# Another load order in the prologue and another order of all steps, in a kernel that adds a long convolution and a gated MLP

## The chip, the cores and the metric

The kernel runs on one NeuronCore of a Trainium2 chip. The metric is the device time of one execution in microseconds. A core has TensorE (PE, matmuls; its weight loads are shown as PEld), VectorE (DVE), ScalarE (ACT), GpSimd (POOL) and SyncE (SP), which here issues nearly all DMA transfers. Each engine works through its own instructions in order; semaphores connect them.

## The reference

S = 2048 positions, D = 640, F = 1728, all in bf16. `xn` is the layer norm of x; the output is the sum of x, a gated long convolution of `k` and `v`, and a gated MLP of `xn`.

```python
x  = A_q
xn = _layernorm(x, axis=-1)
# A: short convolution of k (4 taps), times v, then a causal convolution of length S per channel
k_shift = sum(k_pad[:, t:t + S, :] * shift_k[:, ks - 1 - t] for t in range(ks))
kv = k_shift * v
y  = irfft(rfft(kv, 2 * S) * rfft(ssm_k, 2 * S))[:S] + kv * ssm_D
A  = xn * y
# B: gated MLP
B  = (sigmoid(xn @ w_gate) * (xn @ w_up)) @ w_down
out = x + A + B
```

## The kernel before

**Layout.** Position s = 16 p + b sits on partition p in block b, so x is a tile of 128 partitions x 16 blocks x 640. The MLP goes over four groups of four blocks (512 positions each); the convolution goes over five chunks of 128 channels. The Fourier transform of a chunk is done by matmuls with tables, in two stages with a transposition through DRAM between them, and so is the inverse.

**MLP, per group.** `ln_*` make the statistics and `xn` on VectorE (the power -1/2 on GpSimd); `xn_mm` transposes the blocks on TensorE, `xn_ev` copies them to `xnT` on ScalarE. For each of 13 column blocks `fc` of 128, `gate_mm` and `up_mm` are five matmuls of 512 columns each (lines 257); `gate_ev` is the sigmoid on ScalarE (266), `up_ev` the product into `hT` on VectorE (272). The last 64 columns of gate and up share one product (`both_mm` 278, `both_ev`, `both_mul`, which writes `hT[13]`). `down_mm` (296) multiplies `hT` by `wd`, each output half in two parts of seven matmuls; the second part needs `hT` 7 to 13. `down_ev` (301) adds the result to x.

**Convolution, per chunk c.** `load_h`, `load_halo`, `load_k`, `load_v`, `load_taps` bring `hn`, `kx`, `kvh`, `sraw`. `h_turn` transposes the filter on VectorE, `add_D` adds D on GpSimd, `taps` reorders the taps into `sc`. `kv_op` 0 to 15 (VectorE, 329 to 338) are the short convolution and the product with v, eight steps for each half of the blocks. Then: `st1_mm` 0 to 7 (355, 357) into a PSUM tile, copied by `st1_ev` on ScalarE into a `t1` tile (two steps fill one; there are two `t1` buffers), `wr1` writes `t1` to DRAM (`d1`), `rd2` reads it back as `t2`, `st2_mm` (388), `st2_ev`, `prod` (401, 403), `inv1_mm` (417), `inv1_ev`, `wr2`, `rdb`, `inv2_mm` (456) and `inv2_q`, `inv2_x`, which add the chunk's part to x. `store` writes x to the output.

**PSUM.** Pool psG has four buffers in rotation: gate, up, down, transposed blocks of groups 1 to 3, `psb`. Pool psC has two: stage tiles of the convolution, and the prologue's transposed blocks.

**The prologue (469 to 508).** x's block 0 is loaded on SP's queue, block 1 and then blocks 2 and 3 on ScalarE's; the first 256 columns of `w_gate` on SP's and of `w_up` on ScalarE's, columns 256 to 512 of both on SP's. `busy(15)` issues 15 matmuls of 512 columns on a tile of zeros, whose result nobody reads. Four blocks go through statistics and `xn` on VectorE in order; `ln_xn` of block i - 1 stands behind `ln_stats` of block i. `turn(i)` transposes block i and copies it. For group 0 the products of column blocks 0 and 1 are done in quarters, one for each block as it comes: `quarter(u, fc, i)`, with u = 0 for gate and 1 for up.

**The order of everything else.** `chains` holds a list of steps for each letter; `ORDER` is a string of letters, and each letter issues the next step of its list. So `ORDER` sets the order of the instructions on every engine. The letters: `m` and `n` the loads listed at 540 to 562 (SP); `Z` and `t` taps; `g` MLP matmuls, `s` sigmoids, `u` VectorE's part of the MLP; `l`, `P`, `e`, `E` layer norm, its power, transposition and copy; `H`, `D`, `k` filter, D and `kv_op`; `a`, `A`, `w` stage 1, its copy and its write; `r`, `b`, `B`, `p` read back, stage 2, its copies and the spectral product; `c`, `C`, `W`, `R`, `d`, `q` the inverse; `h`, `K`, `V`, `T` loads of later chunks; `o` stores.

**Transfers in flight.** The trace shows eight semaphores for the transfers of SP and ScalarE in rotation; a transfer is issued when the one eight places before it has landed.

Of the kernel before, what the change touches and what calls it, by code (L numbers as in the profile page):

```python
# [22 lines left out]
NFC = 14  # L23
# [34 lines left out]
def kernel(  # L58
# [410 lines left out]
    sync.dma_start(x[:, 0, :], xr[:, 0, :])  # L469
    nc.scalar.dma_start(x[:, 1, :], xr[:, 1, :])  # L470
    nc.scalar.dma_start(x[:, 2:4, :], xr[:, 2:4, :])
    for u in range(2):
        load_w((sync, nc.scalar)[u], 0, 256, u)
# [15 lines left out]
    busy(15)  # L489
# [10 lines left out]
    for i in range(4):  # L500
        for fc in range(2):
            for u in range(2):
                quarter(u, fc, i)
            if (i, fc) in ((0, 0), (1, 0), (1, 1)):
                turn(1 + i + fc)
# [34 lines left out]
    for k in ((load_w, sync, 512, 768, 0),  # L540
              (load_w, sync, 512, 768, 1),
              (load_taps, 0),
              (sync.dma_start, SMt[:], SMd.ap()),
              (load_w, sync, 768, 1024, 0),
              (load_w, sync, 768, 1024, 1),
              (load_w, sync, 1024, 1280, 0),
              (load_w, sync, 1024, 1280, 1),
              (load_wd, sync, 0, 7),
              *ks(0),
              (load_w, sync, 1280, FF, 0),  # L550
              (load_w, sync, 1280, FF, 1),
              *hs(0),
              *vs(0),
              (load_wd, sync, 7, NFC),
              (sync.dma_start, S1t[:], S1d.ap()),
              *hs(1),
              (load_x, sync, 1),
              *ks(1),
              *vs(1)):
# [62 lines left out]
    mmmmmmmmmmZgmgsmgumgsmgugsgugsmgugskgkugkskgumkgsmkgumkgsmTguHgsHDgumgskkgukgskmgukgskgumkgkmgmutmkm  # L622
    auTaAHgAHDagAwlhauaAlglaglguwlgkPkgAulgAllleKeuKwEekaEekaEgkEVVHAgAHDgwughkgkugkskguKrrkaskaAgkAkguw
    gkskgutkgTskgkKuKaksaAKkgAkaugAwkaksaAkgkwakAgVuAVHasgwHDAauhgAkgkskwbugBrkgBkktbgpBrTkgBpsapsaAuguA
    apKgKswAkaugAkaKkwsakgVHAVgAuDHgswkcugCkgkskCgnuWakaAkgAkgukwbguBrlgBlgulbgBrlgBuglkPpgnulgllleenuEe
    kbEeprgEEgptkBgupBgkaauAgpAkapgswAkaugAkawksaAgkAkguwlcsglCgClbusgrlBWgBkugslpPkaauAgllAlglspwbgBruR
    kgBkscpguCpgCksWbkgBrugBkksbpgBrudBpdgsRqpcqgCqugCqpsWbgBrukgBspbgBrupdBadqsaApRgqAqapgwAqauseeEueaE
    egEEgAgAwaudAdqgwqRqcugCqgCguWbgBrgBugpbpdBrdqgBuqgqpcqgCupgCguWbgBrgBugpspRbgBrugBspcguCpgsCguWbsdr
    BdqgRBqqguqbpsgrBpgBugpspcgCugCsWbguBrdBgqspbqgBupgBspgucpsdCgRqRCqguWbsgBgBugpspgudsdqcqgCqoqdCudqg
    WqqgsqgugoguRRguggugguogodudqogqqogqdoudqogqqogqguogoouo  # L630
    """
    left = {k: iter(v) for k, v in chains.items()}
# [34 lines left out]
```

## Time and profile before

| | us |
|---|---|
| median of 3 runs | 239.67 (239.56 to 239.82) |
| profiled execution, device time | 239.41 |
| its span, first to last instruction | 237.6 |
| TensorE busy | 231.4 |
| VectorE busy | 190.3 |
| ScalarE busy | 141.2 |

The span is the part that the trace shows; about 1.8 us of the device time lie around it.

A row of the profile names the source line, the engine, the operation, what it writes and reads, and its time; a row in order of time begins with its start and its length. "Issue to landing" of a transfer is the time from the instruction on the queue to the semaphore that tells of the last byte. The page's groups give these durations: a product of 512 columns takes 1.08 us for five matmuls, one part of a down block 0.95, a transposed block 0.28, a step `a` 0.45.

### The profile page before, as it was taken

The numbers are of one execution on the slowest core, as the hardware profiler recorded it, in microseconds if no ns is written. First come the engines' busy times: TensorE is split into PE (matmuls) and PEld (weight loads), VectorE is DVE, ScalarE is ACT, GpSimd is POOL, SyncE is SP. The second block draws the span as 40 slices with busy tenths as digits, with TensorE's granted clock in tenths as the row PEclk, the third lists the DMA queues.
The fourth block names the chain that finished last, engine by engine and source line by source line (L and its number), as shares of the span: only waits on it lengthen the run. The fifth ranks groups of instructions, "written<-read, shape, count | busy, mean of one in ns | idle before, by whom it ended". The sixth has DMA issues, their size and how long they took to land.

```text
span 237.6 us, 5553 instructions
## 1 busy us (share of the span) xinstructions
PE 231.4 (97%) x2265; PEld 135.1 (57%) x2265; DVE 190.3 (80%) x350; ACT 141.2 (59%) x178; POOL 11.2 (5%) x24
## 2 busy tenths in 40 slices
PE   8799999999999999999999999999999999999994
PEld 2564445878556455667754434577664434456782
DVE  3633889999999999999999999865585695968372
ACT  2342331728559897864888887997558858764000
POOL 4210000020000000002001000000000000000000
PEclk9999999999999999999999999999999999999999
DMA  7999999889998999999444888975939795285674
GB/s 212 292 314 233 259 322 298 183 249 284 253 311 243 253 295 297 284 267 319 148 183 152 234 230 258 227 228 203 241 109 222 186 281 123 89 238 144 196 237 134
DMA packets 88975, 54.82 MB, mean 231 GB/s; under 512 B 47670, under 2 KB 83062, under 8 KB 88694
## 3 DMA queue, kind: packets, MB, share of 16 engines
q1 hardware_dynamic: 88006, 53.66, 80.8%
q10 hardware_dynamic: 944, 0.82, 1.1%
q8 instruction: 17, 0.28, 0.5%
q14 instruction: 8, 0.07, 0.1%
HBM read 36.12 MB, written 18.35 MB: 229 GB/s over the span
## 4 chain that ended last, share of the span: by engine, by line
PE 95%; DMA 3%; ACT 0%; DVE 0%; ACTq 0%; issue 0%
PE pd L296 26%; PE pg L257 23%; PE pu L257 23%; PE psb L456 4%; PE ps L357 4%; PE ps L355 4%; PE ps L388 3%; DMA w<-in_B_w_up_dram 3%; PE psa L417 2%; PE pg L278 2%; PE pt L234 2%; PE pu L248 1%; PE pg L248 1%; ACT xnT L223 0%; DVE x L301 0%; ACT L119 0%
## 5 line engine op out<-in xcount | busy, mean ns | idle before, releaser
L257 PEld LDWEIGHTS <-w 128*128 128x128 bf16 x500 | 46.5, 98 | 54.3 <-issue 5.3
L296 PE MATMUL pd<-wd,hT 128*128 128x320 bf16 x448 | 64.3, 299 | 0.0
L257 PE MATMUL pg<-xnT,w 128*128 128x512 bf16 x250 | 62.2, 379 | 0.0
L257 PE MATMUL pu<-xnT,w 128*128 128x512 bf16 x250 | 62.1, 379 | 0.0
L296 PEld LDWEIGHTS <-hT 128*128 128x128 bf16 x448 | 42.8, 98 | 17.8 <-issue 1.7
L266 ACT ACTIVATE sig<-pg 128x512 bf16<-128x512 f32 x52 | 31.3, 605 | 30.1 <-PE pg L257 28.2
L272 DVE TENSOR_TENSOR hT<-sig,pu 128x512 bf16<-128x512 bf16 x52 | 35.2, 679 | 14.7 <-PE pu L257 9.3
L223 ACT CAST t<-ps 128x1024 bf16<-128x1024 f32 x40 | 39.1, 1023 | 11.4 <-DMA d<-t 6.3
L223 ACT CAST xz<-ps 128x1024 bf16<-128x1024 f32 x40 | 38.6, 1018 | 10.6 <-PE ps L388 10.5
L301 DVE TENSOR_TENSOR x<-pd,x 128x320 bf16<-128x320 f32 x32 | 15.4, 480 | 15.8 <-PE pd L296 15.7
L403 DVE TENSOR_TENSOR xz<-xz 128x2048 bf16<-128x2048 bf16 x20 | 24.4, 1220 | 0.2
L357 PE MATMUL ps<-kvh,S1t 128*128 128x128 bf16 x160 | 21.2, 219 | 0.0
L335 DVE TENSOR_TENSOR acc<-acc,tmp 128x1024 bf16<-128x1024 bf16 x30 | 20.7, 689 | 0.7
L355 PE MATMUL ps<-kvh,S1t 128*128 128x128 bf16 x160 | 21.2, 217 | 0.0
L333 DVE TENSOR_TENSOR tmp<-kx,sc 128x1024 bf16<-128x1024 bf16 x30 | 20.6, 687 | 0.4
L223 ACT CAST ao<-psa 128x1024 bf16<-128x1024 f32 x16 | 15.6, 1014 | 5.6 <-PE psa L417 3.5
L461 DVE TENSOR_TENSOR yx<-psb,xn 128x512 bf16<-128x512 f32 x20 | 13.8, 691 | 3.9 <-PE psb L456 2.9
L355 PEld LDWEIGHTS <-S1t 128*128 128x128 bf16 x160 | 15.5, 97 | 2.3
L357 PEld LDWEIGHTS <-S1t 128*128 128x128 bf16 x160 | 15.3, 96 | 2.3
L223 ACT COPY xnT<-pt 128x640 bf16<-128x640 bf16 x16 | 10.2, 709 | 10.8 <-PE pt L234 10.5
L198 DVE BATCH_NORM_STATS2 st<-x 128x6 f32<-128x320 bf16 x32 | 13.7, 471 | 2.8 <-DMA x<-in_A_q_dram 2.8
L401 DVE STREAM_SHUFFLE xz<-xz 128x512 f32<-128x512 f32 x20 | 14.6, 728 | 0.0
(44 smaller groups left out, 146.1 us busy)
## 6 DMA issues: line engine op xcount, KB each, us to landing
d<-t SPq DMA_DIRECT2D x20, 512.0 KB, 3.7
t<-d SPq DMA_DIRECT2D x20, 512.0 KB, 4.9
bi<-d SPq DMA_DIRECT2D x8, 512.0 KB, 5.5
d<-ao SPq DMA_DIRECT2D x6, 512.0 KB, 4.1
kx<-in_A_k_dram SPq DMA_DIRECT2D x10, 256.0 KB, 5.0
hn<-in_A_ssm_k_dram SPq DMA_DIRECT2D x20, 128.0 KB, 6.0
kvh<-in_A_v_dram SPq DMA_DIRECT2D x10, 256.0 KB, 5.2
x<-in_A_q_dram SPq DMA_DIRECT2D x3, 640.0 KB
```

Source lines behind the costliest of these rows:

```text
L223: nc.scalar.copy(out=out, in_=in_)
L257: nc.tensor.matmul(pg[:, :], lhsT=w[:, c, u * UP + fc * P:u * UP + (fc + 1) * P], rhs=xnT[:, :, c, :], start=(c == 0), stop=(c == NC - 1))
L266: nc.scalar.activation(sig[fc][:, :], pgs[0, fc][:, :], ACT.Sigmoid)
L272: nc.vector.tensor_tensor(hT[:, fc, :], sig[fc][:, :], pgs[1, fc][:, :], ALU.mult)
L296: nc.tensor.matmul(pd[:, :], lhsT=hT[:, fc, bb * P:(bb + 1) * P], rhs=wd[:, fc, 320 * half:320 * half + 320], start=(fc == 0), stop=(fc == ...
L301: nc.vector.tensor_tensor(x[:, 4 * t + bb, es], pds[bb, half][:, :], x[:, 4 * t + bb, es], ALU.add)
L333: nc.vector.tensor_tensor(d["tmp"][:, :, :], kx[:, lo + 3 - m:hi + 3 - m, :], sb(m), ALU.mult)
L335: nc.vector.tensor_tensor(d["acc"][:, :, :], d["acc"][:, :, :], d["tmp"][:, :, :], ALU.add)
L355: nc.tensor.matmul(ps[:, i, 0:P], lhsT=S1[:, b, h, :], rhs=cin[c]["kvh"][:, 0, b, :], start=True, stop=True)
L357: nc.tensor.matmul(ps[:, i, P:2 * P], lhsT=S1[:, b, h, :], rhs=hp[:, b // 2, b % 2, :], start=True, stop=True)
L401: nc.vector.stream_shuffle(z[:, 2, :, :].bitcast(F32), z[:, 1, :, :].bitcast(F32), swap)
L403: nc.vector.tensor_tensor(z[:, 1:3, :, :], z[:, 0:1, :, :].to_broadcast((P, 2, 8, P)), z[:, 1:3, :, :], ALU.mult)
```

## The change

The prologue loads blocks 0 and 1 of x in halves of 320 columns, one half on each of the two queues, then the first 256 columns of both weights, then block 2 on SP's and block 3 on ScalarE's queue. `busy(15)` becomes `busy(10)`. For block 0 both gate quarters come before both up quarters, and every `turn(i + 1)` stands after the first quarter of block i. The list of loads `m` has another order: the gate and up weights and the filter of chunk 0 come earlier; x's second group comes before `wd`; `kx` and `v` of chunk 0, the table `S1` and the small table `SM` come later. `ORDER` is another string over the same steps: each letter occurs as often as before.

```diff
--- before.py
+++ after.py
@@ -466,11 +466,13 @@
         nc.vector.tensor_tensor(xs, xs, chunks[c]["yx", m][:, :, :], ALU.add)
 
 
-    sync.dma_start(x[:, 0, :], xr[:, 0, :])
-    nc.scalar.dma_start(x[:, 1, :], xr[:, 1, :])
-    nc.scalar.dma_start(x[:, 2:4, :], xr[:, 2:4, :])
-    for u in range(2):
-        load_w((sync, nc.scalar)[u], 0, 256, u)
+    for b in range(2):
+        for i in range(2):
+            (sync, nc.scalar)[i].dma_start(x[:, b, 320 * i:320 * i + 320], xr[:, b, 320 * i:320 * i + 320])
+    for i in range(2):
+        load_w((sync, nc.scalar)[i], 0, 256, i)
+    for i in range(2):
+        (sync, nc.scalar)[i].dma_start(x[:, 2 + i, :], xr[:, 2 + i, :])
     for u in range(2):
         load_w(sync, 256, 512, u)
 
@@ -486,7 +488,7 @@
         xn_ev(0, i)
 
 
-    busy(15)
+    busy(10)
     for i in range(4):
         ln_stats(0, i)
         if i:
@@ -498,11 +500,11 @@
     turn(0)
     busy(2)
     for i in range(4):
-        for fc in range(2):
-            for u in range(2):
-                quarter(u, fc, i)
-            if (i, fc) in ((0, 0), (1, 0), (1, 1)):
-                turn(1 + i + fc)
+        for k in range(4):
+            fc, u = divmod(k, 2) if i else (k % 2, k // 2)
+            quarter(u, fc, i)
+            if k == 0 and i < 3:
+                turn(i + 1)
     for fc in range(2):
         gate_ev(0, fc)
         up_ev(0, fc)
@@ -539,24 +541,24 @@
 
     for k in ((load_w, sync, 512, 768, 0),
               (load_w, sync, 512, 768, 1),
-              (load_taps, 0),
-              (sync.dma_start, SMt[:], SMd.ap()),
               (load_w, sync, 768, 1024, 0),
               (load_w, sync, 768, 1024, 1),
+              (load_taps, 0),
+              *hs(0),
               (load_w, sync, 1024, 1280, 0),
               (load_w, sync, 1024, 1280, 1),
-              (load_wd, sync, 0, 7),
-              *ks(0),
               (load_w, sync, 1280, FF, 0),
               (load_w, sync, 1280, FF, 1),
-              *hs(0),
+              (load_x, sync, 1),
+              (load_wd, sync, 0, 7),
+              *hs(1),
+              (load_wd, sync, 7, NFC),
+              *ks(0),
+              *ks(1),
               *vs(0),
-              (load_wd, sync, 7, NFC),
               (sync.dma_start, S1t[:], S1d.ap()),
-              *hs(1),
-              (load_x, sync, 1),
-              *ks(1),
-              *vs(1)):
+              *vs(1),
+              (sync.dma_start, SMt[:], SMd.ap())):
         step("m", *k)
     for k in ((load_x, sync, 2), (load_x, sync, 3), (sync.dma_start, TBt[:], TBd.ap())):
         step("n", *k)
@@ -619,15 +621,15 @@
         step("o", store, b, b + 1, 0, DM)
 
     ORDER = """
-    mmmmmmmmmmZgmgsmgumgsmgugsgugsmgugskgkugkskgumkgsmkgumkgsmTguHgsHDgumgskkgukgskmgukgskgumkgkmgmutmkm
-    auTaAHgAHDagAwlhauaAlglaglguwlgkPkgAulgAllleKeuKwEekaEekaEgkEVVHAgAHDgwughkgkugkskguKrrkaskaAgkAkguw
-    gkskgutkgTskgkKuKaksaAKkgAkaugAwkaksaAkgkwakAgVuAVHasgwHDAauhgAkgkskwbugBrkgBkktbgpBrTkgBpsapsaAuguA
-    apKgKswAkaugAkaKkwsakgVHAVgAuDHgswkcugCkgkskCgnuWakaAkgAkgukwbguBrlgBlgulbgBrlgBuglkPpgnulgllleenuEe
-    kbEeprgEEgptkBgupBgkaauAgpAkapgswAkaugAkawksaAgkAkguwlcsglCgClbusgrlBWgBkugslpPkaauAgllAlglspwbgBruR
-    kgBkscpguCpgCksWbkgBrugBkksbpgBrudBpdgsRqpcqgCqugCqpsWbgBrukgBspbgBrupdBadqsaApRgqAqapgwAqauseeEueaE
-    egEEgAgAwaudAdqgwqRqcugCqgCguWbgBrgBugpbpdBrdqgBuqgqpcqgCupgCguWbgBrgBugpspRbgBrugBspcguCpgsCguWbsdr
-    BdqgRBqqguqbpsgrBpgBugpspcgCugCsWbguBrdBgqspbqgBupgBspgucpsdCgRqRCqguWbsgBgBugpspgudsdqcqgCqoqdCudqg
-    WqqgsqgugoguRRguggugguogodudqogqqogqdoudqogqqogqguogoouo
+    mmmmmmgmgsmZmgumTgsmHmguDgHsgmugsgugsgmugsgugsguglmslmgmumgHsguDmHgslhguglsgukmgsmlkPmgumkmgmlmkeguE
+    kgukglkeugEkgklgkuekgElkeguEkgkgkKutaKkaTAkgKkAgukwakaAgkAkaguwkaksgAkkngAuawksaAkgVHVAaugDwHAasgkhA
+    kgukgwsktrguTrkgKskKakKaAugkAakgwlAaskaAugkwlasgVkVkgugHsgHADughskAaugAkwlasgAklgwubsgkrBlkPgBuKkbKs
+    pgBrkKgBptgusTpauaApgAkagslwkAaueakEglnAkelgwEkAlaugVAHVeeuwEDckEgHCgkClgWubkgBrkgBukapaAkgpAgwubkgB
+    rlgBukgpbugpBrgBklgucnspgCkpgCutbWkgBrkgBlsbpguBrpRgBksaspaAgupAagAuwkaslakPAgkwkagAuldlsldAqgRlqwcq
+    ugCqkgCksWbkgBrukgBksbpduBrdpgBqasapAgqqAguwqcpsgCkgCukWbskgrBkgBukbspgrBpRgBuapsaAgpAaugAwasaAeueeE
+    ewaEgEEddAqgRqAqgqwcugCgCugWbugBrdBdqgpbqugBrpgBqguqpcgpCgCugWbugBrgBgupRbspgrBgBugpspcguCgCsWbduBrd
+    qgRBqqgspqbugBrpgBspgucpsgCgCuWbsdBrdqgBqqgupbsgqRBpRgBugpspcguCgCsWbduBdqgBqqodsopdgqqoopgugsqqocou
+    gCqgCsWgugsguggRuRgugguggugdudqgqqoddqgqoqguoqgqoguooguo
     """
     left = {k: iter(v) for k, v in chains.items()}
     for k in "".join(ORDER.split()):
```

## The prediction

> **What bounds the kernel now.** I read the page's busy rows and chain first, then TensorE's waits, then the first 14 us in order of time, then the stretches.
>
> ```profile
> PE 231.4 (97%) x2265; PEld 135.1 (57%) x2265; DVE 190.3 (80%) x350; ACT 141.2 (59%) x178; POOL 11.2 (5%) x24
> PE 95%; DMA 3%; ACT 0%; DVE 0%; ACTq 0%; issue 0%
> ```
>
> TensorE is the bound, and the chain that ended last is 95% TensorE. The one transfer on it (3%) is a load of `w_up`.
>
> ```profile
> PE idle L482 <- DVE hT L117: 1.2, 1, 1.2
> PE pu L248 <- DMA w<-in_B_w_up_dram: 0.6, 1, 0.6
> PE pt L234 <- DVE xn L219: 0.6, 1, 0.6
> PE pg L248 <- ACT xnT L223: 0.6, 2, 0.3
> ```
>
> These are all of TensorE's waits (line, releaser, us, times, longest). All four lines (117, 482, 234, 248) belong to the prologue.
>
> ```profile
> 8.80:14.34 5.54, 5.31 (x90) 5.13 (x91) 1.32 (x6) 2.72 (x5) 1.25 (x3) 1.00 1.17 291
> 14.34:36.00 21.66, 21.66 (x104) 9.87 (x102) 14.56 (x22) 6.48 (x11) 0.42 (x1) 1.00 1.12 283
> 36.00:60.00 24.00, 24.00 (x217) 17.50 (x216) 23.56 (x47) 11.98 (x15) 2.17 (x3) 1.00 0.95 252
> 60.00:75.00 15.00, 15.00 (x112) 8.53 (x111) 14.58 (x24) 9.81 (x13) 0.00 (x0) 1.00 1.00 273
> 157.00:234.40 77.40, 77.36 (x864) 45.56 (x861) 50.98 (x91) 42.30 (x52) 0.00 (x0) 1.00 0.66 189
> 234.40:237.60 3.20, 0.00 (x0) 0.00 (x0) 0.49 (x1) 0.00 (x0) 0.00 (x0) 1.00 0.31 108
> ```
>
> The columns are the stretch, its length, the busy us of PE, PEld, DVE, ACT and POOL, the granted clock, the DMA share and GB/s. From the first full product (14.34 us) to 234.4 TensorE is never idle. So the time is 14.34 us of prologue, 220.0 us of matmuls without a gap, and a tail of 3.2 us (the last addition, 0.49, and one store). The diff changes no matmul after the prologue, only their order. So there are two questions: how much earlier the first product starts, and whether 220 us without a gap survives the new order. The tail is the same in both (last `g`, `u`, `o`).
>
> ```profile
> 3.97 0.89 DVE L198 BATCH_NORM_STATS2 st<-x 128x6 f32<-128x320 bf16 x2 [2.85 <-DMA x<-in_A_q_dram]
> 4.89 0.21 DVE L202 BATCH_NORM_AGGREGATE mv<-st 128x2 f32<-128x12 f32 x1
> 5.21 0.88 DVE L198 BATCH_NORM_STATS2 st<-x 128x6 f32<-128x320 bf16 x2
> 6.04 0.45 DVE L219 TENSOR_SCALAR xn<-x,mv,rstd 128x640 bf16<-128x640 bf16 x1
> 6.71 0.88 DVE L198 BATCH_NORM_STATS2 st<-x 128x6 f32<-128x320 bf16 x2
> 10.35 0.45 DVE L219 TENSOR_SCALAR xn<-x,mv,rstd 128x640 bf16<-128x640 bf16 x1 [0.66 <-POOL rstd L214]
> ```
>
> VectorE waits for block 0 until 3.97, then runs the four blocks' statistics almost back to back. The last `xn` is at 10.35. TensorE starts `turn(0)` at 6.54, the first quarter at 7.78, and the first `up` quarter at 8.81, when `w_up` lands.
>
> **The prologue, step by step.** Block 0 is 164 kB, and today blocks 0 and 1 come side by side on two queues. In halves, both queues carry block 0 first. The trace moves 311 GB/s from 4.0 to 8.8 us, at which 164 kB less ahead of block 0 is 0.53 us: it lands at about 3.45. The first half's statistics can run before the second half lands, so only one statistic (0.47 of the row's 0.89) stands between landing and aggregate: 3.95 instead of 4.89. The rest of the row's spacing follows: block 1's statistics at 4.27, `xn` 0 at 5.10, `turn(0)` at 5.6 (before 6.54).
>
> Block 2 now stands behind the first weights. Block 1 and the two 0:256 loads are 0.16 + 0.66 MB after 3.0 us. At 311 GB/s that is 5.6, then 0.16 to 0.33 MB of blocks 2 and 3 (0.5 to 1.0 us) and some 0.6 us from last byte to landing: 6.7 to 7.2. VectorE would want block 2 at 5.77, so it waits, and `xn` 1 stands behind those statistics in the code. I take 6.65, as block 2 is on the earlier queue. From there to the last `xn` the row has 10.35 - 6.71 = 3.64: 10.3, done 10.75. Then `turn(3)` (0.28), 0.2 until ScalarE sees it, the copy to `xnT` 0.70, and four quarters of 0.28. The sum is 10.75 + 0.05 + 0.28 + 0.2 + 0.7 + 0.05 + 1.12 = 13.15, with 0.1 for queueing at TensorE: first product at **13.25**, a gain of **1.1 us**. If block 2 lands at 7.3 it is 0.45; if it never waits, TensorE's and ScalarE's own chain gives about 12.5, a gain of 1.8. The `up` weights (landing near 6.4) stop deciding. Gate quarters first need nothing more. `busy(10)` instead of 15 takes five matmuls of 0.21 from a stretch in which TensorE waits: no cost by itself. The eighth transfer in flight is now reached by x's block 3, so the weights from 256 on wait for the halves' landings (3.45 on). Their queues hold work until about 6, so that wait is covered; uncovered it would be under 1 us of a load needed 4 us later.
>
> **The new order.** Counted from the first product, TensorE's position is a sum of rows (1.08 a product, 0.95 half a down block, 0.28 a transposed block, 0.45 a step `a`). A stall comes where a producer is later than that position. Three places are close.
>
> First, the second half of the first down block, `hT[13]`: 22 products, both_mm and two down halves, position 26.74, that is 40.0 us. The product `both_mul` now queues on VectorE behind `kv_op` 0 and 1, which wait for `kx` of chunk 0 (before, those ran from 23.85). Position of `kv_op` 0: 37.9. Ahead of it and with it the single SP queue carries 9.6 MB (all gate and up weights 4.4, both parts of `wd` 2.2, x 1.3, `hn` of two chunks 1.05, taps, halo and the first half of `kx` 0.6). By the stretches' rates (150 GB/s to 4.0 us, 311 to 8.8, 291 to 14.34) 3.7 MB are moved by 14.34, the rest at 283 GB/s takes 20.9: 35.2, landed at 36. Slack 1.9; at the slowest loading row, 252, it is 23.5 and 38.5: a stall of 0.6. I take 0.
>
> Second, `v` of chunk 0 (1.7 MB more, at 252 another 6.6: 42.5) for `kv_op` 7, position 44.9: free. `S1` 1.0 MB later is due at 51.6 (before 43.0): free.
>
> Third, step `a` of chunk 2, position 67.8 (81.05 us). It needs a PSUM pair that ScalarE frees with `A` 6 of chunk 1 (0.91 + 0.11), and that waits for a `t1` buffer, so for the landing of chunk 1's second write to `d1`. In front of that write, from chunk 2's `v` on (about 63.2 us), the queue carries 4.4 MB: `v`, two writes, four `hn`, two reads `t2`, taps, halo, `kx` of chunk 3. At 273 GB/s that is 16.2 us, and about 1 us to landing: 80.4, where 80.0 is needed. Between 252 (17.5) and 283 (15.6) the stall is 1.7 or none. The rows of just this kind of traffic are the 60 to 75 ones, so I take **0.3**. Before, `A` 6 never waited there. Behind it on ScalarE stand the gate sigmoids, so each tenth lost is TensorE's.
>
> Elsewhere producers keep about the distance that they had: from step `c` 9 on the positions of both orders differ by 0.2 us (198.95 against 199.13), and the last chunk's `d` is at 212.38 in both.
>
> **Sum.** -1.1 + 0.3 = -0.8 us. The profiled execution took 239.41 (span 237.6, 1.8 around it), so 238.6; the median of the runs shown, 239.67, is 0.26 above it: **238.9**.
>
> **Rivals.** (1) *The front gains more and the middle holds*: block 2 lands before VectorE asks, 12.5: -1.8, 237.9. For it: 128 packets behind 640; against: two weight loads stand ahead. (2) *The gain is handed back*: the SP queue is a transfer behind at `hT[13]` or at chunk 2, and TensorE waits as much as it gained, since both places hang on bytes moved and an earlier start makes them due earlier: 1.1 of stall, 239.65. For it: slack of 0 to 2 us after 36 and 80 us of queueing; against: the old order ran the same bytes at the same rates without one gap. (3) *The queue runs late, slower*: at 250 GB/s from 14.34, `kx` lands at 38.7 (0.8 late), and chunk 1's write 1.8 late: 2.6 of stall less 1.1, 241.2. It decides from 1.6 us of stall, a mean rate of about 260. For it: the 252 row; against: that row holds waits of the queue itself. (4) *The clock falls*: with ten warming matmuls TensorE is idle from about 4.75 to 5.6, and again 0.4 and 0.7 us around the first quarter. The warming matmuls before start 0.43 apart and 0.21 apart from about 4 us; at the lower clock 20 groups of 0.28 become 0.56, of which waiting covers about half: +2.5, 240.3. Against: the granted clock was 1.00 over gaps of 0.57, 0.35 and 0.60.
>
> [...]
>
> **How the numbers follow.** Forecast 0.48 (its own range 238.2 to 239.4), rival 1 0.12, rival 2 0.19, rival 3 0.16, rival 4 0.05. The range 237.9 to 240.8 leaves out the far half of rival 3 and a gain over 1.8. About 0.2% (0.48 us) is what a measurement can tell from no change. Faster: most of the forecast (0.44) and rival 1: 0.56. Same: the rest of the forecast, most of rival 2: 0.22. Slower: rivals 3 and 4 and the edge of 2: 0.22.
>
> **What would show it.** Right: first `st` near 3.45, a wait of `st` for x near 5.8 to 6.7, first L257 matmul near 13.25, no TensorE wait for `up` weights, TensorE's waits after that below 0.5 us. Wrong: `hT L287` or `kx` behind a wait of L296 near 40 us; a wait of L355 for `t L223` near 81 us with `DMA d<-t` ahead of it; matmuls of 0.11 spacing in the quarters.

## The result, and the profile after

The changed kernel took **243.1 us** (median of 6 runs, 241.36 to 244.35), the kernel before on the same chip 239.75 (6 runs, 239.45 to 241.14): a ratio of **1.0129, interval 1.0097 to 1.0161**. It is slower by 3.4 us; 238.9 was forecast, and the time lies outside the range of 237.9 to 240.8. Medians are taken over all runs; a ratio and its interval leave out runs more than 1.5% above the fastest of the same kernel, which below is one run each of "ten warming", "change, warm, mended" and "change, fifteen" (there 245.94).

The profiled execution took 243.57 us with a span of 241.8 (before 239.41 and 237.6). First the page's busy rows and chain, of the changed kernel:

```profile
PE 231.9 (96%) x2260; PEld 134.3 (56%) x2260; DVE 189.6 (78%) x350; ACT 141.2 (58%) x178; POOL 11.5 (5%) x24
PE 74%; DMA 10%; DVE 7%; SPq 4%; ACT 2%; issue 2%; DVEq 0%; ACTq 0%
```

TensorE has the same work (231.9 us against 231.4). But only 74% of the chain is TensorE's, where it was 95%: the rest goes through transfers, VectorE and SyncE's queue. TensorE's waits say where (line, releaser, us, times, longest):

```profile
PE pt L234 <- DVE xn L219: 2.9, 3, 1.4
PE idle L484 <- DVE hT L117: 1.2, 1, 1.2
PE pd L296 <- issue: 0.8, 1, 0.8
PE ps L355 <- ACT t L223: 0.6, 1, 0.6
PE pg L248 <- ACT xnT L223: 0.3, 1, 0.3
PE pd L296 <- DVE hT L272: 0.2, 1, 0.2
```

Lines 296 and 355 had no wait before; nor had line 234 outside the prologue. Behind the wait of line 355 stands ScalarE, which waits for the write of a `t1` buffer to `d1` to land before it fills that buffer again:

```profile
84.17 1.01 ACT L223 CAST t<-ps 128x1024 bf16<-128x1024 f32 x1 [2.14 <-DMA d<-t]
```

VectorE in the prologue (start, duration, what was done, idle time before it):

```profile
3.05 0.89 DVE L198 BATCH_NORM_STATS2 st<-x 128x6 f32<-128x320 bf16 x2 [1.93 <-DMA x<-in_A_q_dram]
...
5.12 0.45 DVE L219 TENSOR_SCALAR xn<-x,mv,rstd 128x640 bf16<-128x640 bf16 x1
...
7.45 0.89 DVE L198 BATCH_NORM_STATS2 st<-x 128x6 f32<-128x320 bf16 x2 [1.57 <-DMA x<-in_A_q_dram]
...
11.25 0.45 DVE L219 TENSOR_SCALAR xn<-x,mv,rstd 128x640 bf16<-128x640 bf16 x1 [0.67 <-POOL rstd L214]
```

Block 0's statistics start 0.92 us earlier than before (3.97). Block 2 has landed only at 7.42, and the last `xn` is at 11.25, where it was at 10.35. The first full product starts at 14.19; before it was 14.34. The stretches, in the columns of the prediction:

```profile
14.34:36.00 21.66, 21.66 (x102) 9.80 (x101) 11.65 (x20) 6.33 (x11) 1.19 (x3) 1.00 1.06 272
36.00:60.00 24.00, 22.21 (x186) 15.42 (x185) 23.25 (x45) 8.15 (x11) 1.62 (x2) 1.00 0.92 209
60.00:75.00 15.00, 15.00 (x115) 8.60 (x113) 14.76 (x23) 10.56 (x15) 0.42 (x1) 1.00 0.85 270
```

TensorE is busy 22.21 of 24.00 us between 36 and 60, and the transfers there run at 209 GB/s instead of 252. VectorE is busy 23.25 of 24.00 (23.56 before): it has next to no idle time there in either kernel, so what comes late in this stretch has little room to catch up.

The difference of the two spans is 4.16 us. Start to start, the distance between two neighbouring matmuls of TensorE is longer than elsewhere for the same pair at 39.40 (by 0.39 us), 43.05 (0.93), 44.08 (0.90), 51.80 (0.21), 85.23 (0.77), 100.0 (0.16) and 105.2 (0.42): 3.8 together. The last store ends 4.05 us after the last matmul starts, before 3.57: another 0.5. Less 0.15 at the start, that is the 4.16.

Behind the first three lies one chain. VectorE between 34 and 44 us:

```profile
34.69 1.10 DVE L315 STREAM_TRANSPOSE kvh<-hn 128x512 f32<-128x512 f32 x1 [1.84 <-DMA hn<-in_A_ssm_k_dram]
35.72 0.65 DVE L272 TENSOR_TENSOR hT<-sig,pu 128x512 bf16<-128x512 bf16 x1
36.28 1.09 DVE L315 STREAM_TRANSPOSE kvh<-hn 128x512 f32<-128x512 f32 x1
...
38.66 0.69 DVE L272 TENSOR_TENSOR hT<-sig,pu 128x512 bf16<-128x512 bf16 x1 [0.28 <-issue]
...
42.25 0.69 DVE L287 TENSOR_TENSOR hT<-sig,pg 64x512 bf16<-64x512 bf16 x1
42.97 0.69 DVE L335 TENSOR_TENSOR acc<-acc,tmp 128x1024 bf16<-128x1024 bf16 x1
43.59 0.44 DVE L219 TENSOR_SCALAR xn<-x,mv,rstd 128x640 bf16<-128x640 bf16 x1
```

`h_turn` of chunk 1 (315) waits until 34.69 for that chunk's `hn`. From there VectorE works almost without a pause (0.28 us). `both_mul` (287) comes at 42.25, and the first `xn` of group 1 behind it at 43.59. TensorE needs the one for the second half of the first down block and the other for its transpose: the waits at 43.05 and 44.08. (For the first the view names no releaser, only "issue"; `both_mul` ends at 42.94, just ahead of the matmul.)

### The profile page after: what moved, and what is told of

Read it like the earlier page. It is cut to its first block, busy times and chain, and to the rows that moved or that the text cites. A ratio compares the mean times of both kernels' runs of the same rounds, so it can differ in the third digit from the quotient of the medians.

```text
span 241.8 us, 5548 instructions
## 1 busy us (share of the span) xinstructions
PE 231.9 (96%) x2260; PEld 134.3 (56%) x2260; DVE 189.6 (78%) x350; ACT 141.2 (58%) x178; POOL 11.5 (5%) x24
## 4 chain that ended last, share of the span: by engine, by line
PE 74%; DMA 10%; DVE 7%; SPq 4%; ACT 2%; issue 2%; DVEq 0%; ACTq 0%
PE pd L296 20%; PE pg L257 18%; PE pu L257 17%; DMA hn<-in_A_ssm_k_dram 4%; DMA d<-t 4%; PE psb L456 4%; PE ps L388 3%; PE ps L355 3%; PE ps L357 3%; PE psa L417 2%; DMA x<-in_A_q_dram 2%; ACT t L223 2%; PE pt L234 1%; DVE st L198 1%; SPq L159 1%
## 5 line engine op out<-in xcount | busy, mean ns | idle before, releaser
L296 PE MATMUL pd<-wd,hT 128*128 128x320 bf16 x448 | 65.5, 299 | 1.0 <-issue 0.8
L296 PEld LDWEIGHTS <-hT 128*128 128x128 bf16 x448 | 42.4, 98 | 19.4 <-issue 4.1
L223 ACT COPY xnT<-pt 128x640 bf16<-128x640 bf16 x16 | 10.7, 701 | 18.1 <-PE pt L234 18.1
L335 DVE TENSOR_TENSOR acc<-acc,tmp 128x1024 bf16<-128x1024 bf16 x30 | 20.5, 682 | 0.3
```

Of the source, the lines that this page charges most:

```text
L223: nc.scalar.copy(out=out, in_=in_)
L296: nc.tensor.matmul(pd[:, :], lhsT=hT[:, fc, bb * P:(bb + 1) * P], rhs=wd[:, fc, 320 * half:320 * half + 320], start=(fc == 0), stop=(fc == ...
L335: nc.vector.tensor_tensor(d["acc"][:, :, :], d["acc"][:, :, :], d["tmp"][:, :, :], ALU.add)
```

## The experiments

Eighteen runs follow, told by their spans too: "first" is the start of the first full product (line 257) in the profiled execution, "last" that of the last matmul, both in us. The kernel before has 14.34 and 234.06, a distance of 219.72. Kernels of one set ran on one chip with the same runs of the kernel before.

| kernel | order | first | last | distance | median | ratio to before, interval |
|---|---|---|---|---|---|---|
| the change | new | 14.19 | 237.74 | 223.55 | 243.1 | 1.0129, 1.0097 to 1.0161 |
| **set A:** old front | new | 14.26 | 236.51 | 222.25 | 242.66 | 1.0131, 1.0097 to 1.0165 |
| new front | old | 13.89 | 235.05 | 221.16 | 242.09 | 1.0099, 1.0074 to 1.0125 |
| `hn` first | new | 14.75 | 236.59 | 221.84 | 242.64 | 1.0122, 1.0092 to 1.0151 |
| x ahead of weights | old | 15.55 | 236.37 | 220.82 | 242.84 | 1.0125, 1.0101 to 1.0150 |
| **set B:** ten warming | old | 14.77 | 234.95 | 220.18 | 241.13 | 1.0061, 1.0045 to 1.0077 |
| new front, warm | old | 15.65 | 235.39 | 219.74 | 240.44 | 1.0038, 1.0024 to 1.0051 |
| block 0 in halves | old | 15.00 | 234.86 | 219.86 | 241.64 | 1.0078, 1.0052 to 1.0104 |
| order mended | new | 14.97 | 236.76 | 221.79 | 241.71 | 1.0088, 1.0069 to 1.0107 |
| **set C:** quarters alone | old | 13.80 | 234.84 | 221.04 | 239.82 | 1.0007, 0.9983 to 1.0030 |
| change, warm | new | 15.00 | 238.19 | 223.19 | 243.94 | 1.0174, 1.0147 to 1.0201 |
| change, warm, mended | new | 14.77 | 238.39 | 223.62 | 244.5 | 1.0164, 1.0133 to 1.0196 |
| quarters, `w_up` earlier | old | 14.81 | 234.84 | 220.03 | 240.53 | 1.0030, 1.0013 to 1.0046 |
| **set D:** x on ScalarE's queue | new | 17.34 | 239.73 | 222.39 | 245.6 | 1.0246, 1.0214 to 1.0278 |
| writes first | old | 13.95 | 234.79 | 220.84 | 240.35 | 1.0037, 1.0005 to 1.0069 |
| the change again | new | 14.73 | 236.25 | 221.52 | 243.31 | 1.0183, 1.0154 to 1.0213 |
| change, fifteen | new | 14.69 | 237.86 | 223.17 | 243.38 | 1.0145, 1.0120 to 1.0169 |
| **set E:** fifteen, `hn` first | new | 14.93 | 238.11 | 223.18 | 243.7 | 1.0154, 1.0121 to 1.0187 |
| fifteen, `hn` first, mended | new | 13.99 | 236.07 | 222.08 | 242.39 | 1.0123, 1.0094 to 1.0153 |

The change itself came out at 1.0129 in one set and 1.0183 in another, with profiled spans 1.5 us apart. So differences of less than some 0.5% between sets are left alone here, and differences within a set are read by the intervals. None of these kernels is shown to be faster than the one before.

### Set A: which half of the change costs

**The old front with the new loads and order** (prologue of before, the two loops of loads and `ORDER` of the change):

> The prologue as before, with the new list of loads and the new order of steps. Theory (middle): the lost time lies after the first product, where VectorE stands in its order in front of the filter hn of chunk 1, and ScalarE later in front of the second write to d1; the new front gains only 0.15 us. Then this takes as long as the changed kernel, about 243 us, with TensorE waits of 2 to 4 us in all after 14.3 us. Rival (front): the thinner warming and the late block 2 cost the time and the clock; then this is within 0.5 us of before, 239.7.

**The new front with the old loads and order:**

> The new prologue with the loads and the order of before. Theory (middle): first product near 14.2 us and no wait of TensorE after it, 239.5 us. Rival (front): about 243 us, with the granted clock below 1.00 in most runs.

Measured: 242.66 and 242.09. So the theory held for the first run and fell for the second, where the rival came nearer. Each half alone costs about 1%, and together they cost no more than the first of them. The runs of the new front fall into two groups by their granted clock. Five with 0.999 or 1.000 took 240.54 to 241.93, five with 0.993 took 242.25 to 243.01. All thirteen runs of the kernel before in this set had 0.999 or more, all four of the old front at least 0.997. So part of the new front's cost is the clock, and the order's cost needs no clock.

**`hn` of chunk 1 ahead of the first part of `wd`**, in the changed kernel (one letter `m` of `ORDER` also stands later, not shown):

```diff
-              (load_wd, sync, 0, 7),
               *hs(1),
+              (load_wd, sync, 0, 7),
```

> The changed kernel with the filter of chunk 1 loaded ahead of the first part of wd (1.12 MB) instead of behind it; one load letter stands later, nothing else moves. Theory (hn): hn of chunk 1 lands about 3 us earlier, near 31.5 instead of 34.66, VectorE's wait of 1.84 us for it goes, and with it TensorE's waits between 39 and 52 us: about 2 us less than the changed kernel, 241. Rival (kx): VectorE then waits for kx of chunk 0 instead, which lands near 39.3 in any case, and the time stays within 0.5 us of the changed kernel.

In its profile three of the four `hn` loads of chunk 1 have landed by 29.50 and no `h_turn` of that chunk waits, the waits at 39.4 and 43.05 are gone, and the longest of TensorE's waits are those at 42.86 (0.44), 50.97 (0.60) and 84.32 (0.68). The time, 242.64, is not told apart from the change's, as the rival says; but VectorE does not wait for `kx`, which was the rival's reason. Two of the four runs had a clock under 0.998.

**Blocks 2 and 3 of x ahead of the first weights** (new front, old order):

```diff
+    for i in range(2):
+        (sync, nc.scalar)[i].dma_start(x[:, 2 + i, :], xr[:, 2 + i, :])
     for i in range(2):
         load_w((sync, nc.scalar)[i], 0, 256, i)
-    for i in range(2):
-        (sync, nc.scalar)[i].dma_start(x[:, 2 + i, :], xr[:, 2 + i, :])
```

> The new prologue with blocks 2 and 3 of x ahead of the first weights, and the loads and order of before. Theory (block 2): VectorE no longer waits for block 2 (7.42 us in the changed kernel, wanted at 5.8), the last xn is near 10.0, the first product near 12.8, and the middle keeps its distance: 238.2 us. Rival (weights): 0.33 MB more ahead of the weights puts the first gate quarter behind its weights, near 7.5, and the first product at 14 or later: 239.5 or more. Second rival: the earlier start is taken back by waits in the middle, 239.7.

Here TensorE waits 2.5 us for `w_up`, until 10.86, and the first product comes at 15.55. In kind that is the first rival's reading. It is what is put behind that comes late: block 2 in the change, `w_up` here.

### Set B: the warming, block 0, and two places of the order

**Ten warming matmuls in the kernel before**, and nothing else:

```diff
-    busy(15)
+    busy(10)
```

> The kernel before with ten warming matmuls instead of fifteen and nothing else. Theory (the thinner warming alone lets the granted clock fall): TensorE is then idle from about 5.0 until turn(0) at 6.5, and some of the runs show a clock of 0.990 to 0.993 and a time of about 241.3 (239.5 plus the 1.7 that separates the two groups of runs of the new front), the rest stay at 239.5; median 239.5 to 241.3. Rival (the clock falls because of the later gaps between the transposed blocks, which this kernel does not have): all runs at 239.5 and a clock of at least 0.998.

Slower by 1.0061 (1.0045 to 1.0077), some 1.5 us. The clock fell in two of six runs: 0.993 (241.34) and 0.986 (243.99). But three runs at 1.000 took 240.3, 241.02 and 241.24, so the fallen clock is not all of it. The profile is of the fastest: there the warming ends at 5.3, `w_up` lands at 9.20 instead of 8.77, and 0.5 us are lost at line 417. What the other full-clock runs lose isn't shown.

**The new front with its gaps filled** (old order):

```diff
-    busy(10)
+    busy(15)
...
+            if k == 0 and i == 0:
+                busy(5)
             if k == 0 and i < 3:
                 turn(i + 1)
```

> The new front with before's order of the steps, and fifteen warming matmuls ahead of turn(0) and five more ahead of turn(1), where TensorE waited 1.0 to 1.4 us. Theory (gaps in the first 9 us make the clock fall, and the rest of the front's cost is the old order running into late landings): every run at a clock of at least 0.998, and the median falls from 242.1 to that of the undisturbed runs of the new front, 240.5 to 241.9, say 241.0; it stays slower than before by 1.0 to 1.8 because of the waits of L355 near 77 us and L417 near 124 us. Rival (what falls is not tied to the warming): clocks of 0.993 in half of the runs again, median 242.

All seven runs had 0.998 or more, and 1.0099 became 1.0038. The warming gives back more than half of the new front's loss. It stays slower than before. The profile is of the slowest of the seven runs (241.81). It shows no wait behind the first product (its distance, 219.74, is that of before), which the theory had expected; its loss lies in the front, where block 2 lands at 9.01, 1.6 us later than in the change:

```profile
9.01 0.89 DVE L198 BATCH_NORM_STATS2 st<-x 128x6 f32<-128x320 bf16 x2 [3.26 <-DMA x<-in_A_q_dram]
```

**Block 0 alone in halves, with the change's order of the quarters and fifteen warming matmuls** (the edit of the quarters is shown under "quarters alone" in set C):

```diff
-    sync.dma_start(x[:, 0, :], xr[:, 0, :])
+    for i in range(2):
+        (sync, nc.scalar)[i].dma_start(x[:, 0, 320 * i:320 * i + 320], xr[:, 0, 320 * i:320 * i + 320])
     nc.scalar.dma_start(x[:, 1, :], xr[:, 1, :])
```

> The kernel before with only block 0 of x loaded in halves on both queues and the gate quarters of block 0 ahead of its up quarters; block order, queues of everything else, warming and order of the steps as before. Theory (the halves are worth what the prediction said, and the loss of the front comes from blocks 1 to 3 being spread over both queues and standing behind the weights): first statistics near 3.1 instead of 3.97, last xn near 9.6 instead of 10.35, first full product at 13.5 to 13.9, no new wait over 0.3 us behind it, 238.8 to 239.3. Rival (old order is tuned to its start to within 0.2 us, so that any earlier start is handed back as a wait for a landing): first product 13.5 to 13.9, but waits near 77 or 124 us as in the new front, 239.6 to 240.5.

Both expectations fell: the first product came at 15.00. ScalarE issues its load of `w_up`, the fourth on its queue where it was the third (issued at 1.65), only at 3.21, when the first transfers have landed. TensorE waits 1.1 us for it, until 10.31. Four of six runs had a clock of 0.992 or 0.993, with fifteen warming matmuls: the clock can fall without a cut in the warming.

**The new order mended in two places** (old front): group 1's `ln_var` and `ln_xn` ahead of the `kv_op` beside them, chunk 3's `k` loads behind chunk 1's second and third writes to `d1`:

```diff
-    mmmmmmgmgsmZmgumTgsmHmguDgHsgmugsgugsgmugsgugsguglmslmgmumgHsguDmHgslhguglsgukmgsmlkPmgumkmgmlmkeguE
-    kgukglkeugEkgklgkuekgElkeguEkgkgkKutaKkaTAkgKkAgukwakaAgkAkaguwkaksgAkkngAuawksaAkgVHVAaugDwHAasgkhA
-    kgukgwsktrguTrkgKskKakKaAugkAakgwlAaskaAugkwlasgVkVkgugHsgHADughskAaugAkwlasgAklgwubsgkrBlkPgBuKkbKs
+    mmmmmmgmgsmZmgumTgsmHmguDgHsgmugsgugsgmugsgugsguglmslmgmumgHsguDmHgslhguglsgulPkmgsmkmgumlkmgmmkeguE
+    kgulkgkeugEkglkgkuelkgEkeguEkgkgkKutaKkaTAkgKkAgukwakaAgkAkaguwkaksgAkkngAuawksaAkgVHVAaugDwHAasgkhA
+    kgukgwsktrguTrkgskakaAugkAakgwlAaskaAugkwKKKlasgVkVkgugHsgHADughskAaugAkwlasgAklgwubsgkrBlkPgBuKkbKs
```

> Before's front with the new order, in which VectorE's normalised blocks of x (ln_var and ln_xn of group 1) stand ahead of the kv_op beside them, and chunk 3's k loads stand behind chunk 1's second and third writes to d1. Theory (the new order costs time in single places, where a step stands behind others in an engine's or the queue's order): the waits near 42.4 (0.45), 50.1 (0.22) and 83.8 (0.99) of the new order with the old front go, and 242.5 becomes 240.8 to 241.2; what is left are the 0.6 near 104 and 0.16 near 98.6. Rival (the new order demands more transfers per time than the chip gives, so that a wait that is removed comes back later): the sum of waits behind the first product stays within 0.5 of 2.4 us, 242.2 to 242.7.

The waits near 42.4 and 83.8 went, that near 50.1 nearly so (0.18). In their place stand 0.53 at 76.1 and, at 103.3 and 104.2, 0.44 and 0.88. With the 0.16 near 98 that both have, their sum is 2.2 us, beside 2.4 in the unmended order: the rival's reading. The ratio, 1.0088 against 1.0131 from another set, leaves room for a small gain.

### Set C: an earlier start alone, and the whole change kept warm

**The new order of the quarters alone** (old loads, fifteen warming matmuls, old order):

```diff
-        for fc in range(2):
-            for u in range(2):
-                quarter(u, fc, i)
-            if (i, fc) in ((0, 0), (1, 0), (1, 1)):
-                turn(1 + i + fc)
+        for k in range(4):
+            fc, u = divmod(k, 2) if i else (k % 2, k // 2)
+            quarter(u, fc, i)
+            if k == 0 and i < 3:
+                turn(i + 1)
```

> The kernel before with the new order of the quarters alone (turn(i+1) right behind the first quarter, for block 0 both gate quarters ahead of both up quarters); loads, warming and order of the steps as before. Theory (an earlier start that takes nothing from the warming and nothing from the queues is kept): the transposes no longer stand behind the quarter that waits for w_up, so the first full product moves from 14.34 to some 13.6 to 13.9 and the time to 238.8 to 239.1, clock 0.998 or more in every run. Rival (handed back: the old order's waits for landings near 77 and 124 us, seen behind the new front, appear with any earlier start): 239.3 to 239.8, with 0.3 us or more of waits of L355 or L417.

The first product comes at 13.80, 0.54 us earlier, with clocks of 0.997 or more, and the time is that of before: 1.0007 (0.9983 to 1.0030). TensorE's waits in its profile:

```profile
PE idle L482 <- DVE hT L117: 1.2, 1, 1.2
PE ps L355 <- ACT t L223: 0.8, 2, 0.5
PE pg L248 <- ACT xnT L223: 0.3, 1, 0.3
```

The wait of line 355 is new. It comes at 73.8 and 77.6, 60 us behind the place that was won: ScalarE does not refill a `t1` buffer until the write of it to `d1` has landed (it waits 0.66 us for that until 72.73 and 1.35 until 76.50), and an earlier start of TensorE did not make that landing earlier. The write issued at 72.10 landed at 76.41; in the kernel before, the one issued at 72.37 landed at 75.33. In this profile the two waits lose more than was won (a distance of 221.04 for 219.72). The interval of the ratio leaves room for a gain of 0.4 us or a loss of 0.7.

The run with block 0 in halves (set B) differs from this one by the halves alone. It had its first product 1.2 us later and a ratio of 1.0078: the halves cost time here. In the profile that is the late `w_up`, in four of the six runs the clock too.

**The whole change with fifteen and five warming matmuls**, and **the same with the mended order:**

> The whole change, with fifteen warming matmuls ahead of turn(0) and five more ahead of turn(1). Theory (the fallen clock is a cost of its own beside the waits of the new order): clocks of 0.998 or more in every run and 243.1 becomes 241.2 to 241.8, as the same warming took 1.65 off the new front with the old order. Rival (the new order's waits hang on landings and not on TensorE, so what the clock wins is handed back as longer waits): clocks up, time within 0.6 of 243.1.

> The whole change with that warming and with the order in which group 1's ln_var and ln_xn stand ahead of the kv_op beside them and chunk 3's k loads behind chunk 1's writes. Theory (the parts add): 0.95 less than with the warming alone, some 240.5, so that nearly all of the loss has a named place. Rival (the mended places come back as other waits for landings, as part of them did behind the old front): within 0.4 of the run with the warming alone.

The clocks are 0.997 or more in all runs but one (0.991, with the mended order), and the times do not fall: 1.0174 and 1.0164. In both profiles chunk 1's `hn` lands at 35.0 to 35.2 and `both_mul` follows at 42.6 to 42.8. Both theories fell. Taking out the fallen clock, and the two mended places with it, brought the whole change no nearer to the kernel before.

**Block 3 of x behind `w_up`**, with the new quarters:

```diff
-    nc.scalar.dma_start(x[:, 2:4, :], xr[:, 2:4, :])
+    nc.scalar.dma_start(x[:, 2, :], xr[:, 2, :])
     for u in range(2):
         load_w((sync, nc.scalar)[u], 0, 256, u)
+    nc.scalar.dma_start(x[:, 3, :], xr[:, 3, :])
```

> As the kernel before with the new quarters, and block 3 of x loaded behind the first up weights instead of ahead of them, on the same queue. Theory (the first up quarter waits for w_up, 164 kB of x ahead of it are worth 0.4 to 0.5 us, and block 3 still lands before VectorE asks for it near 8.2): w_up lands near 8.4, first product 0.1 to 0.4 earlier than with the quarters alone, 238.6 to 239.0. Rival (block 3 behind weights lands late as block 2 did in the changed kernel, 9 us or later, and the last xn with it): first product 0.3 to 1.0 later than with the quarters alone, 239.3 to 240.

The rival again: block 3's statistics start at 9.66, TensorE waits 1.0 us for its `xn`, and the first product is at 14.81, a microsecond behind that with the quarters alone.

### Set D: the queue of x, the writes, and the clock once more

**Blocks 2 and 3 of x both on ScalarE's queue**, in the changed kernel:

```diff
     for i in range(2):
-        (sync, nc.scalar)[i].dma_start(x[:, 2 + i, :], xr[:, 2 + i, :])
+        nc.scalar.dma_start(x[:, 2 + i, :], xr[:, 2 + i, :])
```

> The whole change with blocks 2 and 3 of x both on ScalarE's queue behind the up weights, so that SyncE's queue carries one block less ahead of its loads. Theory (the middle of the changed kernel waits for landings from SyncE's queue, and the front makes that queue late by a block): loads from w 256 on land 0.4 to 0.6 us earlier, the waits near 39 to 44 us (0.39, 0.93, 0.90) shrink by 0.5 to 1.5 together, and the time is 0.5 to 1.5 below that of the change on the same chip. Rival (what delays is the rate at which transfers land, not their place in that queue): within 0.4 of the change.

Theory and rival both fell: it is 2.3 us slower than the change on the same chip. Block 2 is issued on ScalarE's queue only at 3.19, when the first transfers have landed; it comes at 9.25, and the first product at 17.34. `hn` of chunk 1 landed at 34.31, which is 0.35 earlier than in the change's first profile. All six runs had a clock of 0.984 to 0.993. This profile shows such a fall; the stretches, in the columns of before:

```profile
4.47:7.87 3.40, 1.99 (x15) 0.77 (x13) 1.30 (x5) 0.69 (x1) 1.11 (x2) 1.00 1.11 314
7.87:11.29 3.42, 0.72 (x13) 0.73 (x14) 1.98 (x7) 0.23 (x1) 0.40 (x1) 1.00 1.15 305
11.29:14.71 3.42, 3.42 (x36) 3.42 (x34) 1.38 (x5) 1.15 (x2) 0.70 (x2) 0.50 1.12 260
14.71:18.13 3.42, 3.42 (x51) 2.96 (x50) 0.81 (x2) 1.85 (x3) 0.64 (x1) 1.00 1.12 211
```

From 7.87 to 11.29 TensorE works only 0.72 of 3.42 us. For the next 3.42 us the granted clock is 0.50, and then 1.00 again. Half of 3.42 is 1.7 us of lost work, and half a clock over 3.42 of some 240 us is a mean of 0.993: the clock of the slower group in set A, whose median lies 1.6 us above that of the other.

**Writes to `d1` first** (quarters alone, `ORDER` with the first two reads of `t2` behind chunk 1's first write, chunk 3's `k` loads behind its second):

```diff
-    auTaAHgAHDagAwlhauaAlglaglguwlgkPkgAulgAllleKeuKwEekaEekaEgkEVVHAgAHDgwughkgkugkskguKrrkaskaAgkAkguw
-    gkskgutkgTskgkKuKaksaAKkgAkaugAwkaksaAkgkwakAgVuAVHasgwHDAauhgAkgkskwbugBrkgBkktbgpBrTkgBpsapsaAuguA
+    auTaAHgAHDagAwlhauaAlglaglguwlgkPkgAulgAllleKeuKwEekaEekaEgkEVVHAgAHDgwughkgkugkskguKkaskaAgkAkguwrr
+    gkskgutkgTskgkuaksaAkgAkaugAwKKKkaksaAkgkwakAgVuAVHasgwHDAauhgAkgkskwbugBrkgBkktbgpBrTkgBpsapsaAuguA
```

> The kernel before with the new quarters, the first two reads of t2 issued behind chunk 1's first write to d1, and chunk 3's k loads behind its second. Theory (the earlier start was handed back at 74 and 78 us because ScalarE waits for these two writes to land before it may reuse t1, and they stand behind reads that TensorE needs only near 81 us and loads that VectorE needs only near 85): the waits of L355 at 73.8 (0.37) and 77.6 (0.71) go, 239.0 to 239.4 where before is 239.4 to 239.9, 0.4 to 0.8 below before on the same chip. Rival (the room is taken from the reads or from chunk 3's loads, and TensorE waits for t2 or VectorE for kx instead): within 0.3 of before or slower, with a new wait of L388 or a later one of L355.

```profile
PE ps L388 <- ACT t L223: 0.7, 2, 0.5
79.83 1.93 ACT L223 CAST t<-ps 128x1024 bf16<-128x1024 f32 x2 [2.49 <-DMA d<-t]
```

The waits at 73.8 and 77.6 went, and at 80.9 and 81.8 two of 0.37 and 0.89 us came, at line 388. They are not for the `t2` that this line reads: they end with ScalarE's copies into `t1`, for which ScalarE itself waited 2.49 us. The third write of chunk 1, behind the `k` loads that were moved, was issued at 74.92 and landed only at 79.73, 4.8 us later (3.0 in the kernel before). So it is the same kind of wait, one write on. The distance is 220.84 where it was 221.04, and at 240.35 (1.0005 to 1.0069) the kernel is no faster than before.

**The change again, and the change with fifteen warming matmuls** (`busy(10)` to `busy(15)`):

> The changed kernel itself, beside its variants on one chip. Both theories: a ratio to before of 1.010 to 1.018, some runs with a clock of 0.990 to 0.993.

> The whole change with fifteen warming matmuls ahead of turn(0) as before the change. Theory A (the fallen clock costs about 1.7 us in the runs that show it, whatever comes later): clocks of 0.998 or more, and the median 0.7 to 1.8 below that of the change on the same chip. Theory B (in the whole change TensorE's time in the front is covered, since the middle waits for landings at fixed times): clocks of 0.998 or more, and the median within 0.4 of that of the change.

Five of the six runs of the change show a clock of 0.986 to 0.992; with fifteen none is under 0.998. The medians are 243.31 and 243.38, as theory B has it. The ratios, 1.0183 and 1.0145, lie 0.9 us apart, as theory A has it, but the intervals overlap (1.0154 to 1.0213, 1.0120 to 1.0169). So these runs do not decide between the two; a gain of up to some 1% by the clock isn't excluded. The profile of the change is another this time. VectorE in the same stretch as shown above:

```profile
33.29 1.10 DVE L315 STREAM_TRANSPOSE kvh<-hn 128x512 f32<-128x512 f32 x1
34.42 0.69 DVE L272 TENSOR_TENSOR hT<-sig,pu 128x512 bf16<-128x512 bf16 x1
35.02 1.10 DVE L315 STREAM_TRANSPOSE kvh<-hn 128x512 f32<-128x512 f32 x1
...
41.01 0.69 DVE L287 TENSOR_TENSOR hT<-sig,pg 64x512 bf16<-64x512 bf16 x1
...
42.34 0.44 DVE L219 TENSOR_SCALAR xn<-x,mv,rstd 128x640 bf16<-128x640 bf16 x1
```

The same program: `hn` is there at 32.90 instead of 34.66, the transpose does not wait, and the distance from first to last is 221.52 instead of 223.55. Over the kernels with the new order it is a switch. Counted from the first product, where chunk 1's last `hn` came by 18.2 us (old front 18.0, mended 17.4, `hn` first, x on ScalarE's queue 17.0, the change again 18.2), `both_mul` is at 26.3 (26.1 in every kernel with the old order). Where it came at 20.0 to 20.5 (the change, warm, warm and mended, fifteen), `both_mul` is at 27.6 to 28.1.

### Set E: the named places together, at full clock

**Fifteen warming matmuls and `hn` first**, then **the mended order on top** (the edits of above, combined):

> The whole change with fifteen warming matmuls and chunk 1's hn loads ahead of the first part of wd. Theory (VectorE's in-order wait for hn of chunk 1 holds both_mul and the xn behind it): both_mul 26.3 us after the first product, the waits of 0.1 to 0.9 near 39.6, 43.3 and 44.3 us shrink to some 0.45 in all, and the ratio to before falls from 1.0145 to about 1.008 (1.5 us less), clocks of 0.998 or more. Rival (what hn wins, the loads behind it lose, kx and wd above all): ratio within 0.003 of 1.0145, with waits for wd, kx or v in place of those for hn.

> The same with group 1's ln_var and ln_xn ahead of the kv_op beside them and chunk 3's k loads behind chunk 1's second and third writes to d1. Theory (the named places add up to the loss): the waits near 43, 51 and 84 us go as well, a ratio of 1.003 to 1.006; what stays are those near 76, 98 and 104 us. Rival (each mend comes back at the next place where ScalarE waits for a write to land): a ratio within 0.002 of that of the run with hn ahead.

`both_mul` came 26.3 us after the first product in both, as the theory says. The ratio stayed, as the rival says: 1.0154. Of the waits that the rival named only one for `v` is there, 0.5 us of VectorE's. In the first profile TensorE's waits behind the prologue are now 0.44 at 43.0, 0.72 at 51.4, 1.05 at 85.2, 0.16 at 99.9 and 0.86 at 105.6. That is 3.2 us, with the wait for chunk 1's `hn` gone; those at 85 and 105 have grown from 0.77 and 0.42. With the mended order the ratio is 1.0123 (1.0094 to 1.0153), the waits are 0.50, 0.16, 0.24, 0.69 and 0.88, and nearly two thirds of them lie near 103 us, at line 417 behind ScalarE's `t`. Here the theory (1.003 to 1.006) fell, and the rival's 0.002 is missed by little, with intervals that overlap.

## Why the prediction was wrong

**The front's gain of 1.1 was 0.15,** and in the second profile of the change a loss of 0.39 (first product 14.73). The first steps came out: `turn(0)` at 5.63 (5.6 said), and no wait for the up weights. That `turn(0)` fits so well is in part luck: block 0 came 0.4 earlier than said, and both of its statistics (0.89), not one, stood behind the landing. The step that failed is the landing of block 2. I took 6.65 with bounds to 7.3; it was 7.42, and in the variants with the same loads up to 9.0. The sum of bytes over one mean rate gave a time that the transfers behind two weight loads did not keep. That is 0.77 of the 0.94 us by which the first product is late (14.19 for 13.25); most of the rest is the chain from there to the last `xn`, 3.80 where 3.64 was taken.

**"`busy(10)`: no cost by itself" was wrong.** Alone in the kernel before it costs 1.5 us (1.0045 to 1.0077). I put the rival "the clock falls" at 0.05, since the clock had been 1.00 over gaps of 0.6 us; that it would stay so over the changed kernel's gaps was my estimate, which no run had shown. The longest gap was not in that rival: behind the first quarter TensorE waited 1.44 us for the `xn` of block 1, where 0.7 was said. (That rival's own sum is wrong too: its 2.5 us with the forecast's other terms give 241.4, not 240.3.) The one fall that a profile shows, in set D, came behind 3.42 us with 0.72 us of matmuls and a gap of 2.77 us; whether the one or the other decides was not separated.

**The middle's 0.3 was 3.8, and this step decides the sign.** I costed the stall at the place `hT[13]` at 0 and that at step `a` of chunk 2 at 0.3. Both came, at the consumers that the text named: at line 296 near 39 and 43 us (0.39 for a product of line 272, 0.93 for line 287), and at line 355 behind `t` (0.77 us, at 85), where ScalarE waited for chunk 1's second write to land, as the text has it. At `hT[13]` the transfer was another. I checked `kx` of chunk 0 and not `hn` of chunk 1, whose `h_turn` now stands ahead of `both_mul` on VectorE and holds everything behind it. Rival 3, the queue running late, is the nearest to what happened, at 0.16: the transfers ran at 272 GB/s from 14.34 to 36 and at 209 from 36 to 60, a mean of 239, where it set its limit at 260. But its 241.2 counted two places with 2.6 us, and its first place hung on `kx`. The xn transposes of group 1 (0.90 and 0.21) and line 417 at 105 (0.42) had been left in "elsewhere producers keep about the distance that they had".

**The tail** was taken as the same and is 0.5 us longer in both profiles of the change, with seven stores issued from 232.2 on (before, five from 231.3 on). Over all profiles with the new order it is 3.6 to 4.1 us. What makes the last store land later wasn't tried.

**What stays open.** No single place is the cause of the middle's loss: wherever a wait was taken out, the others grew or new ones came, in both orders. In every profile ScalarE waits for a write to `d1` to land just ahead of each of the late ones, those at lines 355, 388 and 417 from 74 us on. What all profiles with the new order have in common is a longer time from issue to landing of these writes. The page's row for the changed kernel (KB each, median us to landing):

```profile
d<-t SPq DMA_DIRECT2D x20, 512.0 KB, 4.7
```

It is 3.7 in the kernel before, 3.3 to 3.9 in every profile with the old order and 4.5 to 5.4 in every one with the new. Which of the moved loads makes it so was not isolated. The old order of the steps with the new list of loads wasn't tried: `hn` has one buffer, and in that list chunk 1's load stands ahead of `kx` of chunk 0, for which VectorE waits ahead of the `h_turn` that frees the buffer. Nor was the new order of the steps tried with the old list, so the two are not told apart.

## What to carry to other kernels

When time is won at the start of a kernel whose engines hang together by transfers, look at whether the transfers move too: here 0.54 us were won in the profile and no gain was measured, since 60 us later ScalarE waited for a write to land. A margin worked out from bytes and a mean rate said nothing on a landing that moved by 1.8 us from one execution to the next (`hn` of chunk 1, 34.66 and 32.90); list for an in-order engine every load that anything ahead of the critical instruction waits for, not only its own. And warming matmuls that look like idle filler were not free to cut: ten instead of fifteen cost 1.5 us here, and two of six runs had a clock of 0.993 and 0.986.

## What the runs showed of the hardware

- The granted clock fell after a stretch that was not idle: 0.72 us of matmuls in 3.42 us, the longest gap 2.77 us (x on ScalarE's queue, 7.87 to 11.29; 0.50 for the next 3.42 us). Behind two stretches of that length with more work the clock was 1.00: 1.32 us of matmuls in the first profile of the change (4.92 to 8.34, with 1.04 of the gap of 1.44 us), 1.77 with ten warming matmuls (4.87 to 8.29). Whether the work in such a stretch or the gap decides, no run shows. The timed runs in which the changed kernel's clock fell have no profile.
- Warming matmuls start 0.43 us apart at first and 0.21 to 0.22 apart later, and the step does not always come at the same moment: near 4.1 us after the start in the profile of the kernel before and in the first of the change, but with the new front kept warm their weight loads are still 0.43 us apart at 6.70. Fifteen of them end at 5.97 us in the kernel before and at 7.43 with the new front kept warm.
- One program's transfers land at quite different times: `hn` of chunk 1 at 32.90 and 34.66 in two profiles of the change, block 2 of x at 7.42 and 7.86.
